# Start-up of a transformer layer on TensorE: key weight rows in four transfers, two of them on ScalarE's queue, a constant moved behind the feature maps, and the first tile scaled in two halves

## The chip, the cores and the metric

The kernel runs on one core of one Trainium2 chip. The metric is device time in microseconds (us) of one execution. A profiled execution gives the span, from the first to the last instruction, and the trace. Engines go by the profile's names: PE (TensorE's matmuls) and PEld (its weight loads), DVE (VectorE), ACT (ScalarE), POOL (GpSimd) and SP (SyncE, which issues most transfers; SPq and ACTq are the issuing sequencers).

## The reference

One layer on x of 2048 tokens by 512 features, all in float32. `_A_ref` is linear attention with 32 heads of 16 features, `_B_ref` a gated feed-forward block of 1376 features:

```
xn = layernorm(x)
q, k, v = heads(xn @ wqkv)
pq, pk = q @ w_phi, k @ w_phi                       # per head, 16 x 16
phi(p) = concat(softmax(p), softmax(-p))
o = phi(pq) (phi(pk)^T v) / (phi(pq) sum(phi(pk)) + 1e-6)
s = o @ wo
g = silu((relu(xn @ W_gate) * (xn @ W_up)) @ W_down)
out = x + s * g
```

## The kernel before, in words

The tokens are taken in 16 tiles of 128 (`order`, line 219). A tile is normalized, transposed on TensorE in four 128x128 pieces against the constant `ident` (`transpose_x`, line 297), and stored as a high and a low part, each rounded to the matmul's fp32r type: a product is made of three matmuls, low by high, high by low, high by high (`mm3`, line 198). For the gate and up products the blocks of x stand beside sums and differences of blocks, so that seven products do the work of eight (`gate_up`, line 551).

A first stage goes over the 16 tiles (line 1038): key logits `pk`, values `pv`, queries `pq`, and the state `pkv` of the linear attention. A second stage goes over 11 slices of the feed-forward block for each half of the tokens, with the rest of the attention between, and then the output tiles follow. The low parts are subtracted on DVE or POOL, the high parts are copies on ACT.

The order of each engine's work is fixed when the program is built. `InOrder` (line 45) keeps every engine in program order, and `Clock` (line 62) decides by estimated costs where background work (preparing and spilling the feed-forward weights, the queries) is put between the products. All of these operations are recorded at one line, L58, so the profile's groups are told apart by tile names. Transfers issued on SP and ACT take eight semaphores in turn; the program makes a transfer wait until the last one on its semaphore has landed.

The change concerns the start, lines 950 to 1018. `load_x(0)` (line 223) fetches the first tile `xt`. `ident` comes on ACT's queue; on SP's follow the feature maps of all heads as a block diagonal constant (`bd_sb`, named `cb` in the profile), the transposed key weights `wkT` (four rows of 256 KB, rows 0 and 1 in one transfer), the second tile, and then query and value weights and further tiles. `idle` is a tile of zeros on which TensorE does matmuls `pidle` until work arrives; `mhalf` holds -0.5, the exponent of the normalization.

`norm_vector(0)` (line 278) makes mean and variance on DVE (`bs`, `bm`) and the reciprocal root on POOL (`br`); `norm_vector_apply` (line 288) scales the tile to `xn`. `turn` (line 319) transposes it to `pxT` and copies the high part on ACT. `fold` (line 243) multiplies a row of key weights by the feature maps, four matmuls into one bank (`pfold`), so that the key logits need one product; `split` (line 193) then makes high and low part, `wkh` on ACT and `wkl` on DVE. The order on PE is: `pidle`, the four transposes, the folds of rows 0 to 3, `pk` of the first tile, folds of the query weights (`wqT`), the second tile's transposes, and `pv` with the value weights (raw `wvr`, parts `wvh` on ACT and `wvl` on POOL).

`f_load` (line 455) fetches the weights of a feed-forward slice: `rawg` in two transfers of 256 KB and `rawd` in one. For slices 2 and 3 (`AHEAD`) both halves of `rawg` lie in one tile (`two`, line 447).

Of the kernel before, what the change touches and what calls it, by code (L numbers as in the profile page):

```python
# [9 lines left out]
AF = mybir.ActivationFunctionType  # L10
ALU = mybir.AluOpType
AX = mybir.AxisListType

P = 128
S = 2048
D = 512
# [3 lines left out]
KD = D // P  # L20
# [15 lines left out]
AHEAD = (2, 3)  # L36
# [122 lines left out]
def layer_kernel(ctx: ExitStack, tc: tile.TileContext, x, wkT, wqT, wv, wo, wf, cst, out):  # L159
    pace = Clock()  # L160
    nc = InOrder(tc, pace)
# [4 lines left out]
    def ps(shape=(P, 512), name="ps"):  # L166
        return pp.tile(list(shape), F32, tag="ps", name=name)

    def u8(shape, name, dt=F32):
        return sb.tile(list(shape), dt, tag="u8", bufs=B8, name=name)  # L170

    def u4(shape, name, dt=F32):
        return sb.tile(list(shape), dt, tag="u4", bufs=B4, name=name)

    def u2(shape, name, dt=F32):
        return sb.tile(list(shape), dt, tag="u2", bufs=B2, name=name)

    def small(n, name, bufs=3):
        return sb.tile([P, n], F32, tag=name, bufs=bufs, name=name)
# [43 lines left out]
    def load_x(n):  # L223
        b, i = order[n]
        t = b * TPB + i
        X[n] = u2((P, D), "xt")
        nc.sync.dma_start(X[n], x[t * P:(t + 1) * P, :])
# [26 lines left out]
    mhalf = sb.tile([P, 96], F32, name="mhalf")[:, 0:1]  # L254
# [32 lines left out]

    def norm_vector_apply(n):
        xn, xt, mv, rs = XN[n]
        nc.vector.tensor_scalar(xn, xt, mv[:, 0:1], rs, op0=ALU.subtract, op1=ALU.mult)  # L290
        XN[n] = xn

    def cols(n):
# [151 lines left out]
    RAW, FT, WD = {}, {}, {}  # L445

    def two(name, apart):
        if apart:
            return [u2((P, 2, 2, P), name) for c in range(2)]
        t = u4((P, 2, 2, 2, P), name)  # L450
        return [t[:, c] for c in range(2)]
# [1 line left out]
    DONE = set()  # L453

    def f_load(f):
        RAW[f] = two("rawg", f not in AHEAD), u2((P, D), "rawd")
        for c in range(2):
            nc.sync.dma_start(RAW[f][0][c].rearrange("p k s f -> p (k s f)"), wf[f][:, c * 512:(c + 1) * 512])
        nc.sync.dma_start(RAW[f][1], wf[f][:, 1024:])

    def w_pair(name):
# [10 lines left out]
    def f_prep(f, keep=True):  # L472
# [47 lines left out]
        if keep:  # L520
            FT[f], WD[f] = [wa, wb, wc, wd], fd
            nxt = f + 1
            while nxt in AHEAD:
                nxt += 1
            del rg, rd, ta, tb
            if nxt < NF:
                f_load(nxt)
# [422 lines left out]
    wk_raw, wv_raw, wq_raw = u8((P, KD, D), "wkT"), u8((P, KD, D), "wvr"), u8((P, KD, D), "wqT")  # L950
    bd_sb = u2((P, KD, P), "cb")
    ident = sb.tile([P, P], F32, name="ident")
    load_x(0)
    nc.scalar.dma_start(ident, cst[:, KD, :])
    nc.sync.dma_start(bd_sb, cst[:, :KD, :])
    nc.sync.dma_start(wk_raw[:, 0:2, :], wkT[:, 0:2, :])
    nc.sync.dma_start(wk_raw[:, 2, :], wkT[:, 2, :])
    nc.sync.dma_start(wk_raw[:, 3, :], wkT[:, 3, :])
    load_x(1)
    nc.sync.dma_start(wq_raw[:, 0:2, :], wqT[:, 0:2, :])  # L960
    nc.sync.dma_start(wv_raw[:, 0:2, :], wv[:, 0:2, :])
# [3 lines left out]
    for n in range(3, 7):  # L965
        load_x(n)

    idle = u2((P, P), "idle")
    nc.vector.memset(idle, 0.0)
    p = ps((P, P), name="pidle")  # L970
    for _ in range(12):
        nc.tensor.matmul(p, idle, idle, start=True, stop=True)
    nc.vector.memset(mhalf, -0.5)
    zacc = u4((P, H, 2, DH), "zacc")

    WK, WV, WQ = w_tile("wk"), w_tile("wv"), w_tile("wq")
# [4 lines left out]
    def wv_lo(k):  # L981
        add(nc.gpsimd, by_parity(WV[k][1]), even_first(wv_raw[:, k, :]), f32(by_parity(WV[k][0])), ALU.subtract)
    norm_vector(0)
    norm_vector_apply(0)
    px = turn(0, False)
    folds = [fold(WK, wk_raw[:, k, :], k) for k in range(2)]
# [5 lines left out]
    norm_vector(1)  # L992
    folds[1]()
    norm_vector_apply(1)
    pk = project(0, WK, "pk")
    folds = [fold(WQ, wq_raw[:, k, :], k) for k in range(2)]
# [14 lines left out]
    for s in range(2):  # L1011
        exp_part(early, s)
    norm_vector(3)
    norm_vector_apply(2)
    sums_x(1)
    folds[0]()
# [3 lines left out]
    def all_preps():  # L1020
        for f in AHEAD:
            f_load(f)
            yield 30,
            yield from f_prep(f, False)
        f_load(0)
        yield 30,
        for f in range(NF):
            if f not in AHEAD:
                while at[0] < (START[f] if f < 2 else N + f - 1):
                    yield 3,  # L1030
                if f in WO_WITH:
                    wo_fetch(WO_WITH.index(f))
                yield from f_prep(f)
                if f in WO_WITH:
                    yield from wo_prep(WO_WITH.index(f))
# [289 lines left out]
```

## Time and profile before

| | us |
|---|---|
| time, median of 3 runs | 563.09 (562.93 to 563.81) |
| the profiled execution, its own time | 564.6 |
| its span, first to last instruction | 562.8 |
| busy: PE, PEld | 555.9, 465.1 |
| busy: DVE, ACT, POOL | 412.4, 282.3, 416.7 |

The mean granted clock of TensorE over the span is 0.998. The profile's views used here: the page (busy time of each engine, the chain of work that ended last, the costliest groups), the waits (who waited for whom), the timeline (instructions in order of time, with the idle time before them and what ended it, in brackets), the busy time by stretch, and the transfers with their time from issue to landing. Busy time of PE comes from pipelined matmuls whose ends are modelled: a matmul of 389 ns starts some 227 ns after the one before.

### The profile page before, as it was taken

The page shows a single profiled execution, that of the slowest core. Times are in us where ns is not written, and L with a number is a line of the kernel's source. Part 1 is how long each engine was busy: PE and PEld are TensorE (multiplying, and loading weights), DVE is VectorE, ACT ScalarE, POOL GpSimd, SP SyncE. Part 2 cuts the span into 40 slices and gives each one's busy share as a digit, 9 for nine tenths or more (in the row PEclk, how much of TensorE's full clock was granted, in tenths as well). Part 3 has the DMA queues.
Part 4 walks back from the last instruction along what each step waited for, and adds up shares of the span by engine and source line. Part 5 has one row for each costly group of instructions (what it writes and reads, how often), then busy time and mean ns, then how long its engine had stood idle before and what let it go on. Part 6 is the DMA issues. An engine that isn't in the chain of part 4 may idle for free.

```text
span 562.8 us, 8204 instructions
## 1 busy us (share of the span) xinstructions
PE 555.9 (99%) x2620; PEld 465.1 (83%) x2620; DVE 412.4 (73%) x621; ACT 282.3 (50%) x504; POOL 416.7 (74%) x356
## 2 busy tenths in 40 slices
PE   8999999999999999999999999999999999999996
PEld 7888888888888888888888888888888888888885
DVE  4978866677656898999797432799995959684224
ACT  3898787675555446444425251234563644535500
POOL 1689987999888386998889242573779888888375
PEclk9999999999999999999999999999999999999999
DMA  8349999856599828979867999997485766669684
GB/s 294 122 137 257 260 278 292 243 162 188 149 295 314 325 77 278 321 276 315 289 219 230 252 364 418 397 380 272 119 244 169 219 192 206 206 200 263 165 236 183
DMA packets 84538, 137.98 MB, mean 245 GB/s; under 512 B 7824, under 2 KB 34320, under 8 KB 83600
## 3 DMA queue, kind: packets, MB, share of 16 engines
q1 hardware_dynamic: 81040, 125.33, 65.4%
q0 software_dynamic: 3312, 12.06, 11.1%
q8 instruction: 21, 0.34, 0.2%
q14 instruction: 21, 0.17, 0.1%
q10 hardware_dynamic: 144, 0.07, 0.0%
HBM read 76.87 MB, written 52.69 MB: 230 GB/s over the span
## 4 chain that ended last, share of the span: by engine, by line
PE 97%; DMA 1%; DVE 1%; issue 0%; SPq 0%; DVEq 0%
PE py L58 21%; PE pc L58 11%; PE pd L58 11%; PE pa L58 11%; PE pv L58 8%; PE pk L58 8%; PE pq L58 8%; PE pso L58 7%; PE pb L58 5%; PE pkv L58 3%; PE pnum L58 3%; PE pfold L58 1%; PE pxT L58 1%; DMA wkT<-wkT 1%; DVE yk L58 1%
## 5 line engine op out<-in xcount | busy, mean ns | idle before, releaser
L58 PE MATMUL py<-fdh,hh 128*128 128x512 f32 x176 | 68.5, 389 | 0.0
L58 PE MATMUL py<-fdh,hl 128*128 128x512 f32 x176 | 68.5, 389 | 0.0
L58 PE MATMUL py<-fdl,hh 128*128 128x512 f32 x176 | 68.5, 389 | 0.0
L58 PE MATMUL pa<-XT,wa 128*128 128x512 f32 x264 | 67.3, 389 | 0.0
L58 POOL TENSOR_TENSOR hl<-e,hh 128x512 fp32r<-128x512 f32 x22 | 28.5, 1295 | 45.4 <-ACT hh L58 40.4
L58 PEld LDWEIGHTS pa<-XT,wa 128*128 128x128 f32 x264 | 49.5, 188 | 10.2
L58 ACT ACTIVATE hh<-e 128x512 fp32r<-128x512 f32 x22 | 13.9, 633 | 73.1 <-DVE e L58 70.6
L58 DVE TENSOR_TENSOR y<-py,y 128x512 f32<-128x512 f32 x40 | 27.5, 689 | 24.7 <-PE py L58 24.6
L58 PE MATMUL pv<-wvh,XT 128*128 128x512 f32 x128 | 43.5, 401 | 0.0
L58 POOL TENSOR_TENSOR phl<-ek,phl 128x1024 fp32r<-128x1024 f32 x15 | 36.1, 2406 | 9.9 <-ACT phl L58 9.9
L58 PE MATMUL pk<-wkh,XT 128*128 128x512 f32 x128 | 42.4, 392 | 0.0
L58 POOL TENSOR_TENSOR hl<-u,hh 128x512 fp32r<-128x512 f32 x22 | 28.8, 1308 | 17.2 <-ACT hh L58 14.2
L58 POOL TENSOR_TENSOR ez<-eq,zB 128x1024 f32<-128x1024 f32 x16 | 38.7, 2424 | 3.3 <-ACT eq L58 2.7
L58 PE MATMUL pq<-XT,wqh 128*128 128x512 f32 (+1 forms) x144 | 40.3, 366 | 0.0
L58 PEld LDWEIGHTS py<-fdh,hl 128*128 128x128 f32 x176 | 33.0, 188 | 7.0
L58 PEld LDWEIGHTS py<-fdh,hh 128*128 128x128 f32 x176 | 33.0, 188 | 6.9
L58 PEld LDWEIGHTS py<-fdl,hh 128*128 128x128 f32 x176 | 33.0, 188 | 6.8
L58 POOL TENSOR_TENSOR ol<-of,oh 128x512 fp32r<-128x512 f32 (+1 forms) x13 | 19.9, 1552 | 24.2 <-ACT oh L58 15.3
L58 PE MATMUL pc<-XT,wc 128*128 128x512 f32 x132 | 34.9, 392 | 0.0
L58 PE MATMUL pd<-XT,wc 128*128 128x512 f32 x132 | 33.8, 389 | 0.0
L58 PE MATMUL pc<-XT,wb 128*128 128x512 f32 x132 | 33.7, 389 | 0.0
L58 PE MATMUL pd<-XT,wd 128*128 128x512 f32 x132 | 33.5, 389 | 0.0
(161 smaller groups left out, 1580.9 us busy)
## 6 DMA issues: line engine op xcount, KB each, us to landing
zacc<-ek POOLq DMA_DIRECT2D x15, 512.0 KB, 5.8
xts<-XT SPq DMA_DIRECT2D x4, 1792.0 KB
XT<-xts SPq DMA_DIRECT2D x7, 1024.0 KB, 19.6
wa<-ws SPq DMA_DIRECT2D x26, 256.0 KB, 5.4
wb<-ws SPq DMA_DIRECT2D x26, 256.0 KB, 4.3
wc<-ws SPq DMA_DIRECT2D x26, 256.0 KB, 5.1
rawg<-wf SPq DMA_DIRECT2D x22, 256.0 KB, 3.4
ws<-wa SPq DMA_DIRECT2D x22, 256.0 KB, 4.4
```

The costliest lines, as they stand in the source:

```text
L58: return self.tc.keep_in_program_order(op(*a, **k))
```

## The change

```
@@ norm_vector_apply
-        nc.vector.tensor_scalar(xn, xt, mv[:, 0:1], rs, op0=ALU.subtract, op1=ALU.mult)
+        for c in [slice(0, 256), slice(256, D)] if n == 0 else [slice(0, D)]:
+            nc.vector.tensor_scalar(xn[:, c], xt[:, c], mv[:, 0:1], rs, op0=ALU.subtract, op1=ALU.mult)
@@ f_load
-        RAW[f] = two("rawg", f not in AHEAD), u2((P, D), "rawd")
-        for c in range(2):
-            nc.sync.dma_start(RAW[f][0][c].rearrange("p k s f -> p (k s f)"), wf[f][:, c * 512:(c + 1) * 512])
+        if f == AHEAD[-1]:
+            t = u4((P, 2, 2, 2, P), "rawg")
+            RAW[f] = [t[:, c] for c in range(2)], u2((P, D), "rawd")
+            nc.sync.dma_start(t.rearrange("p c k s f -> p (c k s f)"), wf[f][:, :1024])
+        else:
+            RAW[f] = two("rawg", f not in AHEAD), u2((P, D), "rawd")
+            for c in range(2):
+                nc.sync.dma_start(RAW[f][0][c].rearrange("p k s f -> p (k s f)"), wf[f][:, c * 512:(c + 1) * 512])
@@ start
+    idle = u2((P, P), "idle")
+    nc.vector.memset(idle, 0.0)
+    nc.vector.memset(mhalf, -0.5)
     load_x(0)
-    nc.scalar.dma_start(ident, cst[:, KD, :])
     nc.sync.dma_start(bd_sb, cst[:, :KD, :])
-    nc.sync.dma_start(wk_raw[:, 0:2, :], wkT[:, 0:2, :])
-    nc.sync.dma_start(wk_raw[:, 2, :], wkT[:, 2, :])
-    nc.sync.dma_start(wk_raw[:, 3, :], wkT[:, 3, :])
+    nc.sync.dma_start(ident, cst[:, KD, :])
+    for k in range(2):
+        nc.sync.dma_start(wk_raw[:, k, :], wkT[:, k, :])
+    nc.scalar.activation(small(1, "lm"), mhalf, AF.Copy)
+    for k in range(2, KD):
+        nc.scalar.dma_start(wk_raw[:, k, :], wkT[:, k, :])
     load_x(1)
...
-    idle = u2((P, P), "idle")
-    nc.vector.memset(idle, 0.0)
     p = ps((P, P), name="pidle")
-    for _ in range(12):
+    for _ in range(11):
         nc.tensor.matmul(p, idle, idle, start=True, stop=True)
-    nc.vector.memset(mhalf, -0.5)
```

`ident` goes from ACT's queue to SP's, third behind the tile and the feature maps. The key weights come as four transfers of one row each: rows 0 and 1 on SP, rows 2 and 3 on ACT, behind the load of ACT's function table, which now stands first on ACT, and a copy of one column of `mhalf`. The first tile is scaled in two halves of 256 columns, so that the first two of its four transposes wait for the first half alone; each fold waits for its own row. There are 11 idle matmuls instead of 12 (two passes each). In slice 3 of the feed-forward weights one transfer of 512 KB takes the place of two. In the built program the order of all other instructions on every engine is the same as before.

## The prediction

> **What bounds the kernel now.** I read the page first (busy shares and chain), then TensorE's waits, then the busy time by stretch, then the chain and the timeline of the first 12 us.
>
> ```profile
> span 562.8 us, 8204 instructions
> PE 555.9 (99%) x2620; PEld 465.1 (83%) x2620; DVE 412.4 (73%) x621; ACT 282.3 (50%) x504; POOL 416.7 (74%) x356
> PE 97%; DMA 1%; DVE 1%; issue 0%; SPq 0%; DVEq 0%
> ```
> ```profile
> PE pidle L58 <- DVE mhalf L58: 1.1, 1, 1.1
> PE pfold L58 <- DMA wkT<-wkT: 0.6, 1, 0.6
> PE pxT L58 <- DVE xn L58: 0.4, 1, 0.4
> ```
> ```profile
> 1.06:7.30 6.24, 5.26 (x29) 4.86 (x29) 1.58 (x4) 1.82 (x2) 0.56 (x1) 1.00 0.84 261
> 7.30:170.00 162.70, 162.70 (x856) 139.17 (x857) 121.29 (x190) 117.81 (x226) 137.84 (x134) 1.00 0.76 223
> 170.00:340.00 170.00, 170.00 (x762) 141.23 (x762) 135.69 (x205) 76.00 (x142) 124.09 (x114) 1.00 0.81 274
> 340.00:555.10 215.10, 215.10 (x955) 177.26 (x955) 149.85 (x216) 86.71 (x136) 151.19 (x103) 1.00 0.75 241
> ```
>
> The columns of the last fence are the stretch and its length, then the busy time of PE, PEld, DVE, ACT and POOL with their counts, the granted clock, the DMA share and GB/s. TensorE is busy in every part of the 547.8 us from 7.30 to 555.10, at clock 1.00, and waits three times in all, each time before 7.30. So the end is set by two things: when the stream of useful matmuls starts, and how long that stream is. The change leaves the stream as it is (the only matmuls taken away are two passes of idle ones that warm the clock) and works on its start.
>
> ```profile
> 1.66 5.51 DMA wkT<-wkT
> 7.16 0.14 issue
> 7.30 3.81 PE pfold L58 x32
> ```
> ```profile
> 0.74 0.40 ACTq L58 DMA_DIRECT2D ident<-cst  x1
> 0.75 0.39 SPq L58 DMA_DIRECT2D xt<-x  x1
> ...
> 1.18 1.28 ACT L58 ACT_TABLE_LOAD   x1 [1.18 <-PEq L1317]
> 1.19 0.42 SPq L58 DMA_DIRECT2D cb<-cst  x1
> 1.66 1.37 SPq L58 DMA_DIRECT2D wkT<-wkT  x3
> ...
> 3.69 0.70 DVE L58 BATCH_NORM_STATS2 bs<-xt 128x6 f32<-128x512 f32 x1 [2.67 <-DMA xt<-x]
> ...
> 4.63 0.15 DVE L58 TENSOR_SCALAR br<-bm 128x1 f32<-128x1 f32 x1
> ...
> 5.47 0.55 DVE L58 TENSOR_SCALAR xn<-xt,bm,br 128x512 f32<-128x512 f32 x1 [0.68 <-POOL br L58]
> ...
> 6.07 0.66 PE L58 MATMUL pxT<-ident,xn 128*128 128x128 f32 x4 [0.41 <-DVE xn L58]
> ```
>
> The chain of waits starts with the first transfer of key weights: issued at 1.66, landed 5.51 later at 7.16, and the first fold starts at 7.30. The other path to that point is the first tile: it lands at about 3.69, is scaled by 6.02, is transposed from 6.07, and would let the fold start at about 6.57 (four transposes 0.11 apart, next one behind). Here it has 0.73 us in hand. A fold takes a row of weights: four rows from 7.30 to the start of pk at 10.86 (below), 0.89 each.
>
> **The change part by part.**
>
> *The constant `ident` behind the feature maps.* It leaves ScalarE's queue, where it moved beside the first tile, and comes third on SyncE's.
>
> ```profile
> 1.90:2.30 0.40, 0.40 (x4) 0.40 (x4) 0.00 (x0) 0.40 (x1) 0.00 (x0) 1.00 0.63 92
> 2.30:3.30 1.00, 1.00 (x6) 1.00 (x6) 0.00 (x0) 0.16 (x1) 0.00 (x0) 1.00 1.00 344
> 3.30:3.90 0.60, 0.60 (x5) 0.60 (x4) 0.21 (x1) 0.00 (x0) 0.00 (x0) 1.00 1.05 397
> 3.90:5.40 1.50, 1.50 (x13) 1.50 (x12) 0.82 (x3) 0.00 (x0) 0.53 (x1) 1.00 0.85 238
> 5.40:7.20 1.80, 0.92 (x7) 0.49 (x5) 0.55 (x1) 0.43 (x1) 0.03 (x1) 1.00 0.98 332
> 7.20:8.70 1.50, 1.40 (x12) 1.43 (x13) 0.69 (x1) 0.40 (x2) 0.00 (x0) 1.00 1.00 371
> ```
> ```profile
> cb<-cst SPq DMA_DIRECT2D x1, 256.0 KB, 3.1
> ```
>
> Its 66 kB at 344 GB/s took 0.19 us of the engines while the first tile moved. The tile lands between 0 and 0.19 earlier; I take 0.15. `ident` itself then lands behind the feature maps (issued 1.19, landed 3.1 later, at 4.3), which no more bytes precede than before, so by 4.5; the first transpose wants it after 5.6. That cover is 1 us, so it costs nothing.
>
> *First tile scaled in two halves.* No row shows a 128x256 scaling. It lies between the 0.15 of a 128x1 one and the 0.55 of the whole; halfway is 0.35, the second starting where the first ends. Then the first half is done 0.20 before the whole was, its two transposes hide beside the second half, and the second half ends 5.47 + 0.70 = 6.17 instead of 6.02. Of the four transposes two are left behind it: next matmul at 6.17 + 0.05 + 2 x 0.11 = 6.44 instead of 6.57. The gain is 0.13; if the halves cost 0.28 each, it is 0.27, and if each cost 0.55, it is a loss of 0.27. With `ident`, the tile's path ends at about 6.3.
>
> *Eleven idle matmuls for twelve.* Two passes less. They end at 5.66 now (6.07 less 0.41 of idle time), ahead of the first transpose in either case, and TensorE's clock stands at 1.00 in all the rows. Price 0.
>
> *Key weights.* Before: 512 KB (rows 0 and 1), then two of 256 KB, all on SyncE. After: rows 0 and 1 as two transfers of 256 KB on SyncE, rows 2 and 3 on ScalarE, behind the table load and a one-column activation. SyncE still has seven issues of 0.4 to 0.5 us before the first value weights, so nothing behind is issued later for it. On ScalarE the load (1.28) starts about 0.4 earlier, as no issue stands ahead of it, and ends near 2.05; the activation waits for the half constant, which DVE sets long before it needs the tile, and one column costs about the 0.15 that it costs on DVE. So the issues come at about 2.1 (row 0), 2.25 (row 2), 2.5 (row 1), 2.7 (row 3): row 0 first, and row 2 close behind. What queues on ScalarE behind these issues is the copy of the first transposed tile, after 6.3; even an issue held up by 2 us is covered.
>
> Landings, from the rates above. By 3.90 the engines had moved 37 + 344 + 238 = 619 kB, by 5.40 976 kB, by 7.16 1,560 kB. Before the last byte of the old 512 KB transfer stand 1,114 kB (tile, `ident`, maps, itself), which by these sums were moved at 5.82; it landed at 7.16. It was 1.34 us late, since some engines ran ahead with later transfers while others lagged. For the new ones I count the bytes in order of issue: row 0 is through at 852 kB, 4.88; row 2 at 5.82; row 1 at 1,376 kB, 6.60; row 3 at 1,638 kB, 7.37. To each comes a lateness between 0 and the 1.34 measured; nothing tells which, and I take the half, 0.67: rows 0, 1, 2, 3 at 5.55, 7.27, 6.49, 8.04. Then, with the 0.14 between landing and start:
>
> - fold 0 at 6.3 (the tile's path; the row is there at 5.69)
> - fold 1 at 7.41 (its row; fold 0 would allow 7.19)
> - fold 2 at 8.30 and fold 3 at 9.19 (rows there at 6.63 and 8.18)
>
> Fold 1 started at 7.30 + 0.89 = 8.19 before, so the stream comes 0.78 us earlier. With no lateness fold 1 is at 7.19, a gain of 1.0; with all of it, at 8.08, a gain of 0.1.
>
> The Trainium skill, "ScalarE: Activation LUTs", section "What ACT_TABLE_LOAD costs", gives 1283 ns for the load, as the row here, and about 1380 ns more for a drain. No row here shows the drain, since the next activation came 4 us later. By that rule rows 2 and 3 would be issued at 3.6 and not at 2.25, behind row 1, and the sum would come to the 1.0 of the second rival.
>
> *One transfer for the two halves of weight slice 3.* Same bytes, one issue less, in the stretch where TensorE never waits. It restores the turn of the transfer semaphores that the extra key transfer shifts. In between, some waits name another transfer, long landed. Price 0, at most a few tenths either way.
>
> *Does the start carry to the end?* What doesn't move with TensorE is what waits for transfers.
>
> ```profile
> 10.86 0.47 PE L58 MATMUL pk<-wkh,XT 128*128 128x512 f32 x1
> ...
> 20.12 0.39 PE L58 MATMUL pv<-wvl,XT 128*128 128x512 f32 x1
> ```
> ```profile
> 16.27 1.14 ACT L58 ACTIVATE wvh<-wvr 128x512 fp32r<-128x512 f32 x2
> ```
> ```profile
> 16.97 2.55 POOL L58 TENSOR_TENSOR wvl<-wvr,wvh 128x512 fp32r<-128x512 f32 x2 [1.08 <-ACT wvh L58]
> ```
> ```profile
> DMA to landing us min/median/max: 7.9/8.3/8.6
> ```
>
> The last row is that of the value weights; the second of them, issued at 7.18, landed 8.6 later at 15.8. Their copies at 16.27 can move up by 0.47 and not by 0.78; the low parts then end at 19.05 on GpSimd instead of 19.52. The last product that uses them would stand at 20.12 - 0.78 = 19.34, still 0.3 behind. So the start carries through, and from there every row shows TensorE full.
>
> **Sum.** 0.78 off the profiled execution (span 562.8, run 564.6) gives a span of 562.0 and a run of 563.8; its 1.8 us around the span are not touched. That run stands 1.5 above the median of 563.09 (562.93 to 563.81), so against the median: 562.3.
>
> **The rivals.**
>
> *Rows arrive late all the same (563.0).* The transfer stays 1.34 us behind its share, fold 1 starts at 8.08, gain 0.1. For it: the bytes and the engines are the same, and the stretch from 3.90 to 5.40 moved only 238 GB/s with nothing but these loads in flight. Against it: row 0 is 262 kB fewer bytes than the pair.
>
> *Rows in time, and more (562.0 and below).* Lateness goes, or rows 2 and 3 come behind row 1; the tile's path alone sets the start, 1.0 less, and with halves at 0.28 each 1.1 to 1.2 less. For it: the path has 0.73 in hand now and gets up to 0.46 shorter. Against it: every row must then land near the even share, which the only measured one missed by 1.34.
>
> *Slower: row 1 last (563.75).* ScalarE's queue takes turns with SyncE's from row 2's first byte, which can fall while the feature maps still move; then rows 2 and 3 are both through when row 1 is, at 1,638 kB: 7.37, and with the full lateness 8.71. Fold 1 starts at 8.85 instead of 8.19, and folds 2 and 3 behind it: 0.66 slower. It decides from the point where row 1 lands after 8.05. For it: two transfers of the old order stood behind the pair that TensorE wants first, now they stand beside it. Against it: the issue order above, with row 2 last but for 0.25 us.
>
> By the Trainium skill, "DMA: Bandwidth & Descriptors", section "Queues, rings and completion order", each DMA engine takes turns between the queues it has work for; by that rule row 1 would land with rows 2 and 3, which is this rival with a lateness between 0 (fold 1 at 7.51, still a gain) and 1.34. The trace of before has two queues at once only for `ident`, too small to show it.
>
> **How the numbers follow.** Forecast (fold 1 0.4 to 1.1 us earlier) 0.43, at 562.3; in time and more 0.24; late all the same 0.16; row 1 last 0.17, of which 0.1 for a lateness beyond the measured one or a stall further on that takes it past 564.2. A bound of 0.2% is 1.13 us, about what a measurement of this kernel tells from no change: faster by more 0.25, slower by more 0.10, between them 0.65. The range runs from 561.6 (1.5 us gain: all of the tile's path, and a few tenths of the waits behind) to 563.7 (row 1 last at the measured lateness); some 0.1 is left out on each side.
>
> **What would show it.** Right: the timeline has the first fold near 6.3 with the transposes in two pairs, TensorE's wait for the key weights before fold 0 gone and a short one before fold 1, pk from about 10.1, and the same distance kept to the last matmul. Wrong: fold 1 at 8.1 or later (late, or last), a first tile that lands no earlier, halves that cost over 0.4, or a stream from pk to the last matmul that is longer than before by more than 0.2 us.

## The result and the profile after

The changed kernel takes 566.66 us (median of 6 runs, 565.69 to 568.30) against 563.35 (562.93 to 563.93) of the kernel before: ratio 1.0054, 95% interval 1.0039 to 1.0068. That is about 3 us slower, and outside my range of 561.6 to 563.7. The profiled execution took 565.69 with a span of 563.9, at a granted clock of 0.999. It is the shortest of the six, while the profiled one of the kernel before (564.6) is longer than each of the six behind that kernel's median, so this pair of profiles shows 1.1 us of the 3. After the last matmul the kernel before takes another 4.9 us in its profile and the changed one 3.6, which hides part of what comes before.

First the page's rows on busy time and on the chain, then TensorE's waits (us in total, times, longest).

```profile
span 563.9 us, 8204 instructions
PE 557.9 (99%) x2618; PEld 465.6 (83%) x2618; DVE 412.5 (73%) x622; ACT 283.1 (50%) x505; POOL 416.0 (74%) x356
PE 98%; DMA 1%; DVE 0%; SPq 0%; issue 0%
```
```profile
PE pxT L58 <- DMA ident<-cst: 1.3, 1, 1.3
PE pidle L58 <- DVE mhalf L58: 1.1, 1, 1.1
```

The kernel is bound as before: the start, then a full stream. TensorE is busy 2.0 us longer than before, with two fewer (idle) matmuls. And at the start it no longer waits for key weights; it waits for the constant of the transpositions. The chain of waits and the timeline of the first 8 us:

```profile
1.65 5.57 DMA ident<-cst
7.22 0.14 issue
7.35 0.63 PE pxT L58 x4
7.98 3.79 PE pfold L58 x32
```
```profile
0.74 1.28 ACT L58 ACT_TABLE_LOAD   x1 [0.74 <-PEq L1327]
...
1.07 0.89 ACTq L58 DMA_DIRECT2D wkT<-wkT  x2
1.18 0.42 SPq L58 DMA_DIRECT2D cb<-cst  x1
1.65 0.42 SPq L58 DMA_DIRECT2D ident<-cst  x1
2.04 0.20 ACT L58 ACTIVATE lm<-mhalf 128x1 f32<-128x1 f32 x1
2.11 0.91 SPq L58 DMA_DIRECT2D wkT<-wkT  x2
...
5.12 0.73 DVE L58 TENSOR_SCALAR xn<-xt,bm,br 128x256 f32<-128x256 f32 x2 [0.68 <-POOL br L58]
```

Read the rows of the table load and of ACTq together. ScalarE's two key transfers are issued at 1.07, while the table load still runs and before the small activation at 2.04: both stand ahead of them in the program, and neither holds them. They go out ahead of the feature maps and the constant. The maps, issued at 1.18, land 5.2 us later (3.1 before); the constant, issued at 1.65, lands 5.57 later, at 7.22. The scaled tile was there at 5.85. So fold 0 starts at 7.96 instead of 7.30, 0.66 late. One pair of profiles doesn't measure this: with the start of before, fold 0 begins between 6.72 and 8.14 in eight profiles (the kernel before, and runs 1, 7 to 9 and 12 to 14 below). The constant is the firmer sign: in those eight it landed between 3.84 and 4.01.

In this pair of profiles the larger part of the loss lies far from the edit. The costliest groups, the kernel before first (the last columns are busy us, mean ns of one, idle time ahead), then the changed one:

```profile
L58 PE MATMUL py<-fdh,hh 128*128 128x512 f32 x176 | 68.5, 389 | 0.0
...
L58 PE MATMUL pso<-woh,oh 128*128 128x512 f32 x60 | 23.3, 389 | 0.0
```
```profile
L58 PE MATMUL py<-fdh,hh 128*128 128x512 f32 x176 | 68.6, 390 | 0.0
...
L58 PE MATMUL pso<-woh,oh 128*128 128x512 f32 x60 | 23.8, 396 | 0.0
```

The output products `pso`, which the change doesn't touch, take 396 ns on average instead of 389, in each of three forms of 60; `py` takes what it took. From fold 0 to the end of the last matmul the stream is 552.34 us (7.96 to 560.30) against 550.59 before (7.30 to 557.89): 1.75 longer. The output products give 1.3 of it (180 of 512 columns times 7 ns); those of 256 columns give none (280 to 281 ns after 282 to 283). The products `pnum` (48 of 512 columns) and `pz` (4) of the attention slow down like them and give some 0.3 more, 24 of them here before and after:

```profile
L58 PE MATMUL pnum<-pTh,XT 128*128 128x512 f32 x24 | 9.3, 389 | 0.0
```
```profile
L58 PE MATMUL pnum<-pTh,XT 128*128 128x512 f32 x24 | 9.5, 397 | 0.0
```

The last 0.2 isn't told apart.

What `pso` has to do with the edit is seen in the built programs. The small activation's target, `small(1, "lm")`, is now allocated ahead of the first buffer of 4 KB; it has three buffers that take 32 bytes each. A group of equal buffers is placed where its first member is allocated, so the whole group (`u4`: the attention output's parts `oh` and `ol`, `pTh`, `pTl`, `zh` and others) stands 96 bytes later in every partition, from 191488 to 191584. A matmul has two operands in these buffers or elsewhere: the stationary one, a block of 128x128 (the profile's LDWEIGHTS rows), and the moving one of 256 or 512 columns. In `pso` the moved buffer (`oh`, `ol`) is the stationary operand; in `pnum` and `pz` it is the moving one, and their stationary operands (in `XT`, and `ones`) still start at multiples of 256 bytes.

### The profile page after: what moved, and what is told of

It is laid out like the page before. It is cut to its first block, busy times and chain, and to the rows that moved or that the text cites. A ratio compares the mean times of both kernels' runs of the same rounds, so it can differ in the third digit from the quotient of the medians.

```text
span 563.9 us, 8204 instructions
## 1 busy us (share of the span) xinstructions
PE 557.9 (99%) x2618; PEld 465.6 (83%) x2618; DVE 412.5 (73%) x622; ACT 283.1 (50%) x505; POOL 416.0 (74%) x356
## 4 chain that ended last, share of the span: by engine, by line
PE 98%; DMA 1%; DVE 0%; SPq 0%; issue 0%
PE py L58 21%; PE pc L58 11%; PE pd L58 11%; PE pa L58 11%; PE pso L58 8%; PE pv L58 8%; PE pk L58 8%; PE pq L58 8%; PE pb L58 5%; PE pnum L58 3%; PE pkv L58 3%; PE pfold L58 1%; PE pxT L58 1%; DMA ident<-cst 1%; PE pz L58 0%; DVE yk L58 0%
```

## The experiments

Theory A: two causes, the moved buffers and ScalarE's early transfers. Its first rival, B: the stream is longer because transfers come at other times. Below, "stream" is the time from fold 0 to the end of the last matmul in the profiled execution, and ratios are to the kernel before on the same chip. That kernel itself took between 563.35 and 564.20 in these sets of runs, so the absolute times that were expected can be off by as much, and the ratios decide.

**1. The kernel before, buffers moved by 96 bytes.**

```
     ident = sb.tile([P, P], F32, name="ident")
+    pad = sb.tile([P, 24], F32, name="pad")
```

> The kernel before with one unused tile of 96 bytes per partition placed ahead of the 4 KB buffers, so that all of these start 96 bytes later, as they do in the changed kernel; nothing else differs. Theory A (the addresses of the 4 KB buffers slow the matmuls that read them): pso matmuls at 234 ns instead of 227, the stream from the first fold to the last matmul about 1.7 us longer, 565.0 us. Rival B (the stream is longer because transfers come at other times or wait on other semaphores): pso at 227 ns, 563.3 us.

565.15 us, ratio 1.0026 (1.0014 to 1.0039). The group of `pso`:

```profile
L58 PE MATMUL pso<-woh,oh 128*128 128x512 f32 x60 | 23.8, 396 | 0.0
```

A tile that nothing reads or writes makes the kernel slower by 0.26%, with `pso` at the durations of the changed kernel (398 ns in one of its three forms) and a stream of 552.63. The first cause is shown; B is out for this part.

**2. The changed kernel, buffers back in place.**

```
+    zacc = u4((P, H, 2, DH), "zacc")
     idle = u2((P, P), "idle")
...
-    zacc = u4((P, H, 2, DH), "zacc")
```

> The changed kernel with the first 4 KB buffer allocated ahead of the small one, so that the 4 KB buffers stand where they stood before. Theory A: pso back at 227 ns, the stream as long as before, and only the late start is left (fold 0 near 7.9, +0.66): 564.0 us. Rival B: pso stays at 234 ns, 566.6 us.

`pso` is at 389 ns again, but the time is 566.25 (565.31 to 568.24), ratio 1.0045 (1.0027 to 1.0064): the 564.0 that I expected was wrong. Against the changed kernel's 1.0054 (1.0039 to 1.0068) the time gains nothing that is clear of noise, so the buffers' price in time rests on run 1. TensorE's waits, and the timeline of VectorE, first in this kernel and then in the kernel before:

```profile
PE pxT L58 <- DMA ident<-cst: 1.4, 1, 1.4
PE pidle L58 <- DVE mhalf L58: 1.1, 1, 1.1
PE py L58 <- DVE e L58: 1.0, 1, 1.0
```
```profile
403.06 1.61 DVE L58 SCALAR_TENSOR_TENSOR qd<-qs 128x64 f32<-128x64 f32 x1
```
```profile
402.23 0.37 DVE L58 SCALAR_TENSOR_TENSOR qd<-qs 128x64 f32<-128x64 f32 x1
```

The start is 0.80 late (0.66 in the changed kernel). Then, at 407, TensorE waits 1.0 us for VectorE, which it doesn't in the profile of before: a small operation took 1.61 us instead of 0.37 and ended when a 1.28 us subtraction on GpSimd, begun at 403.30, had ended. The same came in run 9 below. In the other fifteen profiles the same two operations overlap as well and the small one takes 0.36 to 0.37, so an execution can lose a microsecond there, and what decides it isn't shown.

**3. ScalarE's transfers made to wait for the activation** (buffers in place, as in all that follow).

```
-    nc.scalar.activation(small(1, "lm"), mhalf, AF.Copy)
+    for k in range(2, KD):
+        nc.scalar.activation(wk_raw[:, k, 0:1], mhalf, AF.Copy)
```

> As the one with the 4 KB buffers back, and the two small activations write into the first column of key rows 2 and 3, so that ScalarE's transfers of these rows must wait for them. Theory A (ScalarE's transfers went out ahead of the table load and pushed the constant back): rows 2 and 3 issued from about 2.4, constant landed by 5, transposes at 5.6, fold 0 between 6.2 and 7.2, 562.3 to 563.2 us. Rival C (the constant is late because it stands third on SyncE's queue, whatever ScalarE does): transposes still near 7.3, 564.0 us.

565.76 us, ratio 1.0029 (1.0010 to 1.0048). Theory A, as I had put it, fell: the transposes came at 7.02, nearer to rival C's 7.3. The timeline, then stretches (clock, DMA share and GB/s are the last three columns):

```profile
2.27 0.86 ACTq L58 DMA_DIRECT2D wkT<-wkT  x2
...
7.02 0.63 PE L58 MATMUL pxT<-ident,xn 128*128 128x128 f32 x4 [1.64 <-DMA ident<-cst]
...
8.24 4.01 PE L58 MATMUL pfold<-cb,wkT 128*128 128x128 f32 x21 [0.60 <-DMA wkT<-wkT]
```
```profile
3.90:5.40 1.50, 1.48 (x11) 1.28 (x10) 0.75 (x4) 0.00 (x0) 0.56 (x1) 1.00 0.64 155
```
```profile
8.00:9.00 1.00, 0.76 (x3) 0.79 (x4) 0.69 (x1) 0.28 (x1) 0.00 (x0) 0.50 1.09 393
9.00:11.00 2.00, 2.00 (x12) 2.00 (x11) 0.04 (x2) 0.60 (x1) 0.00 (x0) 0.50 1.02 409
```

The transfers do wait now, until 2.27, behind the maps, the constant and row 0. It doesn't help: between 3.9 and 5.4 the DMA engines are busy only 64% of the time, and the constant still lands at 6.9. TensorE's granted clock is 0.50 from 7.8 on, within the second of its two waits, and the folds run at half speed until past 11 (1.85 us for the first, 0.89 for the third). In run 4 below, with waits of 0.80 and 1.66, it stays at 1.00, so the length of the waits alone doesn't tell when it falls. The loss isn't the early issue alone, then. Whether the second queue makes the constant late or its third place on SyncE's, run 5 tells.

**4. The constant first on ScalarE's queue, rows 2 and 3 behind it there.**

```
     load_x(0)
+    nc.scalar.dma_start(ident, cst[:, KD, :])
     nc.sync.dma_start(bd_sb, cst[:, :KD, :])
-    nc.sync.dma_start(ident, cst[:, KD, :])
```

> As the one with the 4 KB buffers back, but the constant is the first transfer on ScalarE's queue again, as before; key rows 2 and 3 follow it there at once. Theory A: transposes at about 5.7, then fold 0 waits for the feature maps (6.3 in the changed kernel) and row 0, 6.9 to 7.8: 562.9 to 563.8 us. Rival C: the same, so this run tells what the constant's place alone is worth.

564.70 us, ratio 1.0016 (1.0000 to 1.0031).

```profile
6.06 0.76 PE L58 MATMUL pxT<-ident,xn 128*128 128x128 f32 x4 [0.80 <-DVE xn L58]
8.48 3.79 PE L58 MATMUL pfold<-cb,wkT 128*128 128x128 f32 x30 [1.66 <-DMA wkT<-wkT]
```

The transposes are on time; now the maps and row 0 are what comes late, to 8.48, later than I had allowed (7.8).

**5. All four rows on SyncE, the constant third there.**

```
-    nc.scalar.activation(small(1, "lm"), mhalf, AF.Copy)
     for k in range(2, KD):
-        nc.scalar.dma_start(wk_raw[:, k, :], wkT[:, k, :])
+        nc.sync.dma_start(wk_raw[:, k, :], wkT[:, k, :])
```

> The changed kernel with the 4 KB buffers back in place, no small activation, and all four key rows on SyncE behind the constant, in order 0 to 3. Theory A (rows 2 and 3, issued on ScalarE at 1.07, went ahead of the feature maps and the constant): constant landed by 5, transposes at 5.6 in pairs, fold 0 between 6.2 and 7.0, 562.5 to 563.3 us. Rival C (the constant is late by its place on SyncE's queue): transposes not before 6.5, 564 us or more.

564.22 us, ratio 0.9996 (0.9985 to 1.0008). The timeline:

```profile
6.16 1.08 PE L58 MATMUL pxT<-ident,xn 128*128 128x128 f32 x4
7.36 4.04 PE L58 MATMUL pfold<-cb,wkT 128*128 128x128 f32 x32
```

The constant landed 4.4 after its issue at 1.65, at 6.03, and not by 5; the idle matmuls ran until 6.12, so TensorE hardly waited for it. Rival C (transposes not before 6.5) is out as the main cause. Against run 2 only the queue of rows 2 and 3 differs, and with it their turn (the small activation is gone too): 1.0045 (1.0027 to 1.0064) against 0.9996. The intervals don't meet, so the second cause is shown: the two rows on ScalarE's queue. Expected was 562.5 to 563.3 and fold 0 by 7.0; the first row came at 7.22, still late.

**6. As 5, the constant first on ScalarE's queue.** The edit is that of run 4 on top of run 5.

> As the one with all rows on SyncE, but the constant first on ScalarE's queue, as before. So against the kernel before it has the key rows one by one and the first tile in halves, and nothing else at the start. Theory A: transposes at 5.9, fold 0 at 6.5 to 7.2, the stream as long as before: 562.5 to 563.3 us. Rival C: faster than the one with the constant third on SyncE by 0.3 us or more.

563.63 us, ratio 0.9994 (0.9980 to 1.0007).

```profile
5.89 0.76 PE L58 MATMUL pxT<-ident,xn 128*128 128x128 f32 x4 [0.38 <-DVE xn L58]
6.50 3.87 PE L58 MATMUL pfold<-cb,wkT 128*128 128x128 f32 x32
```

Here, with little but single rows and the halves at the start, the profile has a gain of the size that I had worked out: fold 0 at 6.50, 0.80 earlier, the last matmul's end 0.81 earlier (557.08 against 557.89), stream 550.58. The time, expected at 562.5 to 563.3, isn't shown to move. Runs 4 and 6 differ only in the queue of rows 2 and 3 and the activation: fold 0 at 8.48 against 6.50. Against run 5 no gain is shown (0.9994 and 0.9996), where rival C had wanted 0.3 us.

**7, 8, 9, 12, 13, 14. How far the buffers may be moved.** Run 1 with a tile of 32, 64, 128, 256, 512 and 1024 bytes.

> The kernel before with the 4 KB buffers 32 bytes later. Theory A: if the matmuls want them at multiples of 64 bytes, pso at 234 ns as with 96; if the slow case is special to 96, 227 ns. Rival B: 227 ns.

> The kernel before with the 4 KB buffers 64 bytes later. Theory A: 227 ns if multiples of 64 bytes are enough, 234 ns if 128 are wanted. Rival B: 227 ns.

> The kernel before with the 4 KB buffers 128 bytes later. Theory A, now that 32 and 64 were as slow as 96: at a multiple of 128 bytes again, pso back at 227 ns and the stream near 550.6 us. Rival D (not the alignment but any move of these buffers, say against the others, costs it): 233 ns or more.

> The kernel before with the 4 KB buffers 256 bytes later. In the kernel before all operands of the matmuls start at multiples of 512 bytes. Theory G (a stationary operand of 128 float32, 512 bytes, wants to start at a multiple of 512): 232 to 234 ns for pso. Rival H (256 are enough): 227 ns. Rival D (any move costs): 232 ns or more.

> The kernel before with the 4 KB buffers 512 bytes later. Theory G: pso at 227 ns and the stream at 550.6 unless a DVE wait adds to it. Rival D: 232 ns or more.

> The kernel before with the 4 KB buffers 1024 bytes later. Theory G: 227 ns. Rival D: 232 ns or more. A third case: 227 here and not at 512, then 1024 is wanted.

| moved by, bytes | 0 | 32 | 64 | 96 | 128 | 256 | 512 | 1024 |
|---|---|---|---|---|---|---|---|---|
| mean ns of a `pso` matmul (`woh,oh`) | 389 | 396 | 395 | 396 | 395 | 389 | 389 | 389 |
| stream, us | 550.59 | 552.48 | 552.53 | 552.63 | 553.52 | 550.48 | 550.49 | 550.47 |

The rows of 128 and of 256 bytes:

```profile
L58 PE MATMUL pso<-woh,oh 128*128 128x512 f32 x60 | 23.7, 395 | 0.0
```
```profile
L58 PE MATMUL pso<-woh,oh 128*128 128x512 f32 x60 | 23.3, 389 | 0.0
```

(The stream at 128 has the 0.9 us wait for VectorE of run 2; those at 64 and 128 also hold 0.6 and 0.2 of waiting for the last row of key weights.) Multiples of 256 bytes are fast, the four smaller moves are slow. Rival H holds; G, that 512 are wanted, and D, that any move costs, are out, and so is my guess before run 9 that 128 would do. The profiled executions of 256, 512 and 1024, the only ones, took 562.92, 564.38 and 562.91, those of 32, 64 and 128 took 565.98, 564.71 and 566.12; single times carry the start's and the end's variation as well, so the durations decide here.

**10. As 6, with the twelve idle matmuls of before.**

> The version with the key rows one by one on SyncE, the constant first on ScalarE, the tile in halves and the 4 KB buffers in place, with the twelve idle matmuls of before instead of eleven, so that TensorE has less idle time ahead of the first transpose. Theory A: fold 0 at 6.5 again, the stream as before, 0.8 us less than before: 562.5 to 563.4 us. Rival E (the gain of that version's profile was one lucky landing): fold 0 at 7 or later, no different from before.

563.80 us, ratio 1.0003 (0.9993 to 1.0014); 562.5 to 563.4 was expected. Fold 0 at 6.63, early again, which speaks against E (run 15 speaks for it); but of the 0.67 only 0.11 is left at the last matmul. One row of TensorE's waits tells of 0.3:

```profile
PE pso L58 <- POOL ol L58: 0.3, 1, 0.3
```

**11 and 15. As 6, with slice 3 in two transfers again; one profiled execution, then timed.**

```
-        if f == AHEAD[-1]:
+        if f < 0:
```

> The version with the key rows one by one on SyncE, the constant first on ScalarE, the tile in halves, but slice 3 of the feed-forward weights in two transfers as before, which shifts the turn of the transfer semaphores by one. Theory A: the merged transfer is worth nothing, stream from fold 0 to the last matmul 550.6 within 0.2. Rival F (the semaphores' turn makes waits): 551 or more.

> The version with the key rows one by one on SyncE, the constant first on ScalarE, the tile in halves and slice 3 in two transfers, now timed. Theory A: 0.7 to 0.9 us less than before if nothing later takes it back, 562.6 to 563.0 us. Rival I (a later wait of TensorE for DVE, which came in two of the shifted runs at 407, takes it back in many executions): within 0.3 us of before.

562.77 in the one execution; timed 563.69, ratio 0.9996 (0.9987 to 1.0005). Streams of 550.39 and 550.50: the merged transfer is worth nothing, and F is out. Fold 0 was at 6.63 in the one and, waiting for its row, at 7.23 in the other, so E isn't settled. The timed run missed the expected 562.6 to 563.0 and lies within rival I's 0.3, but the wait at 407 that I blames isn't in its profile. Over the four profiles with this start (runs 6, 10, 11, 15) the first key logits begin at 10.12, 10.32, 10.13 and 10.80, with the start of before between 10.65 and 11.70: the start looks earlier, the time doesn't, and where the difference goes isn't known. No version here is shown to beat the kernel before.

## Why the prediction was wrong

- *What bounds the kernel: "when the stream of useful matmuls starts, and how long that stream is".* Right up to the last matmul. What follows it, 3.5 to 4.9 us in these profiles, was left out.
- *"The change leaves the stream as it is."* Wrong, and the step that failed most in the profile: 1.75 us more, some 1.5 of it from 512-column matmuls that read the moved buffers. I went through the order of the instructions and not through where their buffers lie. Run 1 puts a price of 0.26% (0.14 to 0.39) on it alone.
- *Key weights: issues "at about 2.1 (row 0), 2.25 (row 2)".* Wrong. Row 2 went out at 1.07. I let the transfers stand behind the table load and the activation, and the trace shows neither holding them; where a semaphore made them wait for the activation (run 3), row 2 went out at 2.27. The Trainium skill, "Perfetto Trace Analysis", section "DVE / Act Engine Instruction", says that the sequencer hands such an instruction to a wait queue and decodes the next; the issue at 1.07 agrees, and I hadn't weighed it. The drain of 1380 ns behind the table load, by which the prediction would have had the rows at 3.6, doesn't show: the activation starts at 2.04, 0.02 after the load's end.
- *The constant: "it costs nothing", 1 us of cover.* Wrong, and the step that failed at the start: it landed at 7.22, not by 4.5, with the rows of ScalarE's queue beside it, and 6.03 even with them on SyncE (run 5). Counting bytes in order of issue didn't hold with two queues loaded, and even on one the 64 KB came 1.8 us behind that count (the bytes up to and with it had been moved by about 4.2, an estimate from run 5's GB/s, counted as in the prediction).
- *Landings.* The lateness of 1.34 was one execution's. With the start of before the pair of rows landed between 6.21 and 8.00 in eight profiles, and a single row 0 between 5.94 and 7.09 in runs 6, 10, 11 and 15: the start varies by more than the gain that I forecast.
- *The rival "row 1 last".* It has the right sign by luck. Fold 1 came at 8.92, 0.65 later than before (8.27 by the trace, not the 8.19 that I worked out), and the rival says 0.66; but the constant was late and not row 1, and the rows were there when the folds wanted them. I had no rival in which the constant is late.
- *Halves.* Each took 0.41, the second 0.33 after the first, 0.73 in all where the whole took 0.55; I had 0.35 each and 0.70. The sum is right, though "over 0.4" was one of my signs of being wrong.
- *Smaller terms.* The first tile landed 0.36 earlier (3.31 for 3.67; I took 0.15). The eleven idle matmuls ended at 6.06, later than the twelve before (5.67) and after the first half of the tile (5.53); the late constant hid it. And "nothing behind is issued later" is wrong: the first value weights went out at 6.35 instead of 4.03, but TensorE didn't wait for them.
- *Single rows and halves, 0.78 earlier.* Fold 0 came 0.80 earlier in run 6, 0.67 in runs 10 and 11, 0.07 in run 15. The size of run 6 is partly luck, as I had fold 0 at 6.3 and fold 1 waiting for its row, and there fold 0 came at 6.50 and fold 1 waited for nothing. It isn't clear in the time.
- *"From there every row shows TensorE full"*, so a gain would carry through. Mostly: streams stay within 0.2 where buffers are in place, except 1.3 more in run 2 and in run 3 (half clock in the folds), 0.6 in runs 4 and 10 and 0.3 in run 5.

What stays open. Why run 2 is 0.45% slower: its profiled execution, the fastest of its seven, shows 0.8 at the start and about 1.1 at 407; of the slower ones there is no profile. Nor is it settled why two rows on a second queue make the constant late, or why the DMA engines sit partly idle between 3.9 and 5.4 (64 to 89% busy in nine of the seventeen profiles, with either start). And the start varies by itself: in the eight profiles whose start is that of before (the kernel before and the seven moved ones) the first key logits begin between 10.65 and 11.70, and the end follows the last matmul by 3.5 to 4.9 us whichever kernel it is. Differences under 1 us in one profile are therefore not held against a kernel here, and of the 3 us the shares of the two causes are known only as intervals: 0.8 to 2.2 us for the buffers (run 1), 1.5 to 3.6 with the buffers back (run 2).

## What to carry to other kernels

Before counting what an added line costs, look where the allocator puts it: a tile of 4 bytes ahead of a group of buffers moved all of them by 96 bytes, and the matmuls of 512 columns with either operand in them paid some 7 ns each. Moves by multiples of 256 bytes cost nothing here, so keep such groups there. Don't count on an instruction ahead of a transfer in program order to delay the transfer: a table load and an activation on ScalarE didn't, a semaphore did. And when the first microseconds are bound by transfers, rows on a second queue can go ahead of the small thing that everything waits for; in the four kernels here with such rows no fold came earlier than in the kernel before.

## What the runs showed of the hardware that I had not expected

- Matmuls of 512 columns with an operand in buffers moved by 32 to 128 bytes slow down: `pso` (stationary operand there) starts every 232 to 236 ns instead of 227 and takes 395 to 398 ns instead of 389, and `pnum` (moving operand there) takes 397 instead of 389 in the changed kernel. Those of 256 columns don't, and with moves by 256, 512 or 1024 bytes none does. Which property of the address counts beyond that isn't shown.
- A transfer on ScalarE's queue was issued 0.95 us before the end of the table load that stands ahead of it.
- TensorE's clock fell to 0.50 in run 3 at 7.8, between waits of 1.64 and 0.60 us that end at 7.02 and 8.24, with four transposes between, and was back only past 11. In run 4, with waits of 0.80 and 1.66 us, it stayed at 1.00.
- Where rows 2 and 3 went on ScalarE's queue, the Trainium skill, "DMA: Bandwidth & Descriptors", section "Issuing engines are not separate DMA queues", agrees with the runs: it says that a second issuing engine saves no more than issue time, and in no run did they bring a fold forward.
